# Load order of the first tiles and the source of the scaled identities in a fused attention and feed-forward kernel

## The chip, the cores and the metric

One core of a Trainium2 chip. The metric is the device time of one execution in microseconds (us). Single executions of one kernel here scatter by about 0.5 us to either side, a few by more, so times are medians of several. All runs that are compared are of the fast state. The span of a profile (first to last instruction) is 1.8 to 2.3 us shorter than the device time of that execution.

## The reference

```python
# attention: B, H, S, D = 4, 8, 768, 64
scores = q @ k.T / sqrt(D)                       # per head
keep   = (key position < 8) | (0 <= i - j < 96)  # 8 global keys, 96 local ones
scores += -slope[h] * dist                       # slope[h] = 2**-(h+1); dist 96 for global keys outside the band
x = softmax(where(keep, scores, -1e9)) @ v       # then heads side by side: x is 3072 x 512
# feed-forward: w_in 512 x 2048, w_out 2048 x 512
out = relu(x @ w_in)**2 @ w_out                  # float32
```

## The kernel before

The 3072 rows are 24 tiles of 128. For each of the first six tiles TensorE (PE) transposes q and k (for later tiles a DMA does). For every tile it makes scores (for the first three tiles with the bias added by a matmul of a *scaled identity* and the distance matrix), and multiplies the probabilities with v ("pv"). Two tiles make a block, and each block goes through eight slices of w_in ("s1": 8 matmuls per slice) and of w_out ("s2": 4 per slice). The weights are loaded once, a slice at a time. Every load but the q and k of tile 0 is issued by GpSimd and cast from fp32 to bf16 on the way; the same queue carries parts (q, k or v of one tile) and weight slices, and what stands behind waits for what stands ahead.

```python
def swdge(name, dst, src, t):              # one load of that queue
    nc.gpsimd.dma_start(out=dst, in_=src)
    issue[1] = max(issue[1], issue[0] + 3.3) + t
    issue[0] += 0.75 if name[0][0] == "w" else 0.88
    land[name] = issue[1] + 0.3 + min(max(0.1 * (issue[1] - 8), 0.0), 1.6)
...
load_part(0, 1); load_part(1, 1); load_v(0); load_v(1)         # q1 k1 v0 v1
...
for h in range(H):                                             # VectorE
    nc.vector.tensor_scalar_mul(sid[h], ident, float(slopes[h] / scale))
...
for w in "i0 T2 i1 T3 i2 o0 i3 o1 i4 o2 T4 i5 o3 i6 o4 T5 i7 o5 o6 o7".split():
    ...                                    # T: q, k, v of a tile; i: w_in slice; o: w_out slice
for name, at in list(land.items()):
    landed(name, at)                       # planned landing, an input to the static schedule
```

`land` is no more than a plan. When the program is built, a small list scheduler places all work on the engines, using these landing times; the order it finds is fixed. On the chip PE takes its work in this order and waits, by semaphore, for what really has not landed.

The softmax here doesn't subtract the row's maximum and nothing guards it: scores larger than these inputs give would overflow.

## Time and profile before

| what | before |
|---|---|
| device time, 3 runs | 214.84 us (214.77 to 214.9) |
| span of the profile | 213.1 us |
| PE busy | 205.5 us, 96% |
| transfers of GpSimd's queue | 79,200 packets, 13.37 MB |
| first s1 | starts at 14.9 us |
| the last idle time of PE that the profile shows | ends at 25.2 us |

The forty-slice row of PE in the prediction below is full except for the head and the end. A "chain" is followed back from the last instruction, and names at each step what it waited for last. A landing is read as issue time plus the time to landing in the list of DMA issues.

### The profile page before, as it was taken

To read this page: it belongs to the slowest core of one execution; us is meant where nothing else is said; L and a number is where in the kernel's file an instruction comes from. 1 tells how busy PE (TensorE), PEld (TensorE's weight loads), DVE (VectorE), ACT (ScalarE), POOL (GpSimd) and SP (SyncE) were. 2 spreads that over 40 slices of the span, in tenths; PEclk is the share of its full clock that TensorE was granted. 3 is DMA by queue.
4 is the path that set the end of the run, shared out by engine and by line. 5 is a ranking of instruction groups with operands and counts; after the bars stand their busy time and mean duration, and the time that the engine had idled before them with its cause. 6 is when DMAs were issued, how large, how long until landed. Compare 5 with 4: busy or idle time off the path is not lost.

```text
span 213.1 us, 5046 instructions
## 1 busy us (share of the span) xinstructions
PE 205.5 (96%) x1992; PEld 141.2 (66%) x1992; DVE 142.4 (67%) x383; ACT 117.5 (55%) x217; POOL 74.4 (35%) x91
## 2 busy tenths in 40 slices
PE   7968999999999999999999999999999999999994
PEld 3656677655676767666767667666767667676773
DVE  7756668752886768755867957855857857844640
ACT  6848476633763645753654754753754754733541
POOL 8986677531044134314314422422422400000000
PEclk9999999999999999999999999999999999999999
DMA  9999999999899999999999899799999992310202
GB/s 127 140 165 197 182 196 182 178 123 210 185 95 87 218 100 93 189 129 84 203 141 81 180 103 119 154 128 119 192 130 78 152 131 39 123 28 0 98 0 98
DMA packets 113702, 27.58 MB, mean 129 GB/s; under 512 B 104336, under 2 KB 110736, under 8 KB 113680
## 3 DMA queue, kind: packets, MB, share of 16 engines
q0 software_dynamic: 79200, 13.37, 81.4%
q1 hardware_dynamic: 34480, 13.90, 32.7%
q8 instruction: 15, 0.25, 0.5%
q14 instruction: 7, 0.06, 0.1%
HBM read 27.26 MB, written 6.29 MB: 157 GB/s over the span
## 4 chain that ended last, share of the span: by engine, by line
PE 87%; DMA 7%; POOL 4%; issue 0%; ACT 0%; POOLq 0%
PE hT L675 39%; PE acc L745 38%; DMA win<-in_moe_w_in_dram 7%; PE sc L449 5%; PE po L562 4%; POOL qk L193 2%; POOL v L193 1%; PE tr L372 0%; POOL win L193 0%; PE trx L625 0%; ACT o L304 0%; POOL pbi L246 0%; POOLq L246 0%; POOLq L813 0%
## 5 line engine op out<-in xcount | busy, mean ns | idle before, releaser
L675 PE MATMUL hT<-xT,win 128*128 128x256 bf16 x768 | 98.7, 273 | 0.4 <-DMA win<-in_moe_w_in_dram 0.2
L745 PE MATMUL acc<-wout,hs 128*128 128x512 bf16 (+1 forms) x400 | 98.1, 371 | 0.2 <-DMA wout<-in_moe_w_out_dram 0.2
L696 ACT ACTIVATE hr<-hT 128x512 f32<-128x512 f32 x96 | 57.4, 599 | 68.1 <-PE hT L675 67.0
L675 PEld LDWEIGHTS <-win 128*128 128x128 bf16 x768 | 72.8, 98 | 23.9 <-DMA win<-in_moe_w_in_dram 1.6
L708 DVE TENSOR_TENSOR hs<-hr 128x512 bf16<-128x512 f32 x96 | 65.9, 687 | 23.0 <-ACT hr L696 21.7
L745 PEld LDWEIGHTS <-hs 128*128 128x128 bf16 x400 | 36.5, 98 | 24.4 <-issue 0.4
L193 POOL DMA_DIRECT2D qk<-in_q_dram x23 | 20.6, 894 | 87.0 <-DVE qk L346 75.0
L495 ACT ACTIVATE esc<-sc 128x512 bf16<-128x512 f32 x78 | 42.1, 601 | 10.3 <-PE sc L449 10.3
L520 DVE TENSOR_TENSOR at<-esc,E 128x512 bf16<-128x512 bf16 x78 | 32.0, 422 | 8.0 <-ACT esc L495 6.9
L193 POOL DMA_DIRECT2D v<-in_v_dram x24 | 22.2, 924 | 2.4 <-DVE at L520 1.2
L590 DVE TENSOR_TENSOR x<-po,rs 128x256 bf16<-128x256 f32 x48 | 20.4, 425 | 1.7
L193 POOL DMA_DIRECT2D qk<-in_k_dram x23 | 20.5, 892 | 0.3 <-issue 0.2
L562 PEld LDWEIGHTS <-at 128*128 128x128 bf16 x352 | 16.8, 97 | 4.5 <-ACT at L495 0.6
L562 PE MATMUL po<-v,at 128*128 128x65 bf16 x352 | 18.6, 193 | 0.3 <-ACT at L495 0.3
L589 DVE RECIPROCAL rs<-po 128x4 f32<-128x4 f32 x48 | 8.7, 181 | 13.2 <-PE po L562 13.0
L449 PEld LDWEIGHTS <-qkT 64*128 64x128 bf16 x352 | 9.9, 94 | 8.4 <-issue 6.6
L306 DVE COPY o<-acc 128x512 f32<-128x512 f32 x11 | 7.6, 692 | 10.6 <-PE acc L745 10.6
L449 PE MATMUL sc<-qkT 64*128 64x128 bf16 x192 | 13.1, 219 | 0.4 <-DVE qkT L306 0.3
L304 ACT COPY o<-acc 128x512 f32<-128x512 f32 (+1 forms) x14 | 7.8, 555 | 6.7 <-PE acc L745 6.7
L449 PE MATMUL sc<-qkT,qkT 64*128 64x128 bf16 x160 | 11.3, 216 | 0.0
L193 POOL DMA_DIRECT2D win<-in_moe_w_in_dram x8 | 6.4, 794 | 1.7 <-DMA win<-in_moe_w_in_dram 1.1
L495 ACT ACTIVATE at<-sc 128x512 bf16<-128x512 f32 x10 | 5.3, 598 | 2.5 <-PE sc L449 2.5
(41 smaller groups left out, 58.2 us busy)
## 6 DMA issues: line engine op xcount, KB each, us to landing
out_dram<-o SPq DMA_DIRECT2D x23, 256.0 KB, 3.1
v<-in_v_dram POOLq DMA_DIRECT2D x24, 128.0 KB, 5.6
qk<-in_q_dram POOLq DMA_DIRECT2D x23, 128.0 KB, 4.7
qk<-in_k_dram POOLq DMA_DIRECT2D x23, 128.0 KB, 5.4
win<-in_moe_w_in_dram POOLq DMA_DIRECT2D x8, 256.0 KB, 8.6
wout<-in_moe_w_out_dram POOLq DMA_DIRECT2D x8, 256.0 KB, 8.8
qkT<-qk SPq DMA_TRANSPOSE x18, 3.5
xT<-x SPq DMA_TRANSPOSE x18, 3.8
```

Source lines behind the costliest of these rows:

```text
L193: nc.gpsimd.dma_start(out=dst, in_=src)
L304: nc.scalar.copy(dst, src)
L449: nc.tensor.matmul(out=tiles["sc", j, odd, g][:, at, :], lhsT=qkT[(j - kt) % NKT][half, 1, pair, :], rhs=qkT[j % NKT][half, 0, pair, :], s ...
L495: nc.scalar.activation(out=esc, in_=tiles.pop(("sc", j, odd, g)).rearrange("p a c -> p (a c)"), func=Act.Exp, scale=scale,)
L520: nc.vector.tensor_mul(at, tiles.pop(("esc", j, odd, g)), bias)
L562: nc.tensor.matmul(out=po[:, hi, :], lhsT=tiles["at", j, odd, g][:, at * P : (at + 1) * P], rhs=v_sb[kj][:, h, :], start=(i == 0), stop=(i ...
L589: nc.vector.reciprocal(rs, po[:, :, D : D + 1])
L590: nc.vector.tensor_tensor(out=x[:, 4 * hf : 4 * hf + 4, :], in0=po[:, :, :D], in1=rs.to_broadcast([P, 4, D]), op=Alu.mult,)
L675: nc.tensor.matmul(out=hT[:, c, :], lhsT=w_in_sb[s][:, kt, c * P : (c + 1) * P], rhs=tiles["xT", blk][:, kt, :], start=(kt == 0), stop=(kt ...
L696: nc.scalar.activation(hr, tiles.pop(("hT", blk, s)), Act.Relu)
L708: nc.vector.tensor_mul(hs, hr, hr)
L745: nc.tensor.matmul(out=tiles["acc", blk, sub, half], lhsT=hs[:, c, sub * P : (sub + 1) * P], rhs=w_out_sb[s][:, c, cols], start=(s == 0 an ...
```

## The change

Its intent: let the attention of the first four tiles run before any weights are needed, then have each weight slice serve two blocks as it lands; and make the scaled identities without holding GpSimd up. The landing table is fitted anew to the new order. The diff, cut to its core:

```diff
-    issue = [1.0, 5.0]
+    issue = [1.35, 4.6]
...
-        land[name] = issue[1] + 0.3 + min(max(0.1 * (issue[1] - 8), 0.0), 1.6)
+        late = [m for at, m in ((0, 0.5), (8, 0.8), (13.6, 1.9), (36, 2.8)) if issue[1] >= at]
+        land[name] = issue[1] + late[-1]
...
-    load_part(0, 1)
-    load_part(1, 1)
-    load_v(0)
-    load_v(1)
...
-        nc.vector.tensor_scalar_mul(sid[h], ident, float(slopes[h] / scale))
+        nc.vector.scalar_tensor_tensor(
+            out=sid[h], in0=ident32, scalar=float(slopes[h] / scale), in1=ident32,
+            op0=Alu.mult, op1=Alu.mult,
+        )
...
-    for w in "i0 T2 i1 T3 i2 o0 i3 o1 i4 o2 T4 i5 o3 i6 o4 T5 i7 o5 o6 o7".split():
+    for w in "q1 k1 v0 q2 k2 v1 q3 k3 v2 v3 i0 i1 i2 i3 o0 i4 T4 i5 o1 o2 i6 i7 o3 q5 k5 o4 o5 o6 o7 v5".split():
```

It has three parts: the *order* of the loads, the landing *table*, and the *identities*.

More of the change, by code (lines that the diff above doesn't have):

```diff
@@ L207 @@
             plain[n, j] = t_
-            land["qk"[n], j] = 4.15 + 1.1 * n
+            land["qk"[n], j] = 4.1 + 1.1 * n
     def load_v(j):
@@ L288 @@
         ones.update({j: o for j in js})
-    for w in "i0 T2 i1 T3 i2 o0 i3 o1 i4 o2 T4 i5 o3 i6 o4 T5 i7 o5 o6 o7".split():
-        kind, n = w[0], int(w[1:])
-        {"T": load_tile, "i": load_w_in, "o": load_w_out}[kind](n)
+    pieces = {
+        "T": load_tile, "i": load_w_in, "o": load_w_out, "v": load_v,
+        "q": lambda j: load_part(0, j), "k": lambda j: load_part(1, j),
+    }
+    for w in "q1 k1 v0 q2 k2 v1 q3 k3 v2 v3 i0 i1 i2 i3 o0 i4 T4 i5 o1 o2 i6 i7 o3 q5 k5 o4 o5 o6 o7 v5".split():
+        pieces[w[0]](int(w[1:]))
     for name, at in list(land.items()):
```

## The prediction

> **What bounds the kernel now.** I first read the page's busy shares and the row of forty slices, for which engine and when.
>
> ```profile
> span 213.1 us, 5046 instructions
> ...
> PE 205.5 (96%) x1992; PEld 141.2 (66%) x1992; DVE 142.4 (67%) x383; ACT 117.5 (55%) x217; POOL 74.4 (35%) x91
> ...
> PE   7968999999999999999999999999999999999994
> ...
> POOL 8986677531044134314314422422422400000000
> ```
>
> TensorE (PE) is the bound, and is short of work only in the first five slices (27 us) and in the drain of the last store. The change touches nothing after the loads of the first six tiles and the weights, so only the head can move. Next the table by stretches (PE's busy time is the second number):
>
> ```profile
> 4.00:8.00 4.00, 3.74 (x48) 2.75 (x48) 2.46 (x7) 3.52 (x10) 4.00 (x5) 1.00 2.04 137
> 8.00:12.00 4.00, 2.64 (x53) 1.84 (x48) 3.15 (x12) 2.65 (x6) 4.00 (x6) 1.00 1.90 151
> 12.00:16.00 4.00, 3.44 (x52) 2.70 (x52) 2.28 (x23) 1.83 (x4) 3.27 (x5) 1.00 2.08 169
> 16.00:20.00 4.00, 3.33 (x53) 2.46 (x54) 2.31 (x8) 3.12 (x7) 3.25 (x4) 1.00 1.51 195
> 20.00:24.00 4.00, 3.69 (x37) 2.51 (x38) 3.31 (x11) 2.53 (x6) 2.33 (x3) 1.00 1.35 200
> 24.00:28.00 4.00, 3.91 (x31) 2.62 (x30) 2.22 (x6) 2.07 (x4) 2.69 (x4) 1.00 2.03 173
> 28.00:48.00 20.00, 20.00 (x205) 14.27 (x202) 14.56 (x34) 11.93 (x22) 11.27 (x14) 1.00 1.78 168
> ```
>
> From 28 us PE is never idle. Before that busy time flatters it: an isolated block of 4 transposes counts 0.39 us, while in full flow the next block starts 0.23 us later. So I count streaming work. Starts in the timeline between 28 and 45 us give the cost of a block in full flow: 8 first matmuls ("s1" of one weight slice and block of two tiles) 0.87, 4 second matmuls ("s2") 0.86, 4 transposes 0.23, 8 probability-times-v matmuls ("pv", half a tile) 0.24, 16 score matmuls 0.55; 8 bias matmuls take about 0.45. From PE's first transpose (4.41) to 25.22 the kernel does 0.9 (fp32 transposes) + 6 x 0.23 + 5 x 0.45 + 3.5 x 0.55 + 7 x 0.24 + 4 x 0.23 = 9.06 us for the attention of tiles 0 to 3, and 4 s1 (3.48) and 2 s2 (1.72): 14.26 us of work in 20.81. **PE loses about 6.5 us there; this is the ceiling of any gain.** Being 2% faster needs 4.3 us of it.
>
> The chain of waits up to 27 us tells who causes it:
>
> ```profile
> 3.25 2.34 POOL v L193 x2
> 5.59 0.76 POOL win L193
> 6.34 1.76 POOL qk L193 x2
> 8.10 0.82 POOL v L193
> 8.92 7.17 DMA win<-in_moe_w_in_dram
> 16.09 0.28 issue
> 16.37 8.80 DMA win<-in_moe_w_in_dram
> 25.17 0.05 issue
> 25.22 1.81 PE hT L675 x15
> ```
>
> It is the load queue of GpSimd: the issues up to 9 us, then the transfers themselves. The last wait of PE for a load ends at 25.17, with the fifth w_in slice. The queue is a fixed stream: from issue plus time to landing I get w_in slice 2 at 19.9, w_out 0 at 21.2, w_in 3 at 22.6, w_in 4 at 25.2: one weight slice per 1.3 us; a q, k or v part takes 0.85 to 0.95. Two more landings that I use, from the list of DMA issues in narrow windows around their issue (v of tile 3 issued at 11.40, w_out slice 4 at 25.46):
>
> ```profile
> v<-in_v_dram POOLq DMA_DIRECT2D x1, 128.0 KB, 7.4
> ...
> wout<-in_moe_w_out_dram POOLq DMA_DIRECT2D x1, 256.0 KB, 8.8
> ```
>
> They land at 18.8 and 34.3.
>
> **The skill.** "SBUF — State Buffer", section "Who interferes with whom", says that tensor_scalar can take a two-port mode, in which it holds the port pair shared with GpSimd for the whole instruction; that a DMA issued by GpSimd needs GpSimd to write descriptors, so that it stalls meanwhile; and that a two-input op has no such mode. "VectorE: DVE Perf Modes", "What auto-detection actually checks", gives the fast modes to 16-bit, single-source, SBUF-to-SBUF operations. The eight bf16 scaled identities are that. The trace agrees in place and size:
>
> ```profile
> 3.22 2.37 POOL L193 DMA_DIRECT2D v<-in_v_dram  x2
> ...
> 3.40 1.30 DVE L273 TENSOR_SCALAR sid<-ident 128x128 bf16<-128x128 bf16 x8
> ```
>
> Two v issues take 2.37 us where later ones take 0.92 each: 0.53 us lost, beside the eight. "DMA: Bandwidth & Descriptors", "Queues, rings and completion order", says that descriptors of a queue start in ring order on each DMA engine. Landings that follow the issue order at these even steps agree. So the change reorders a stream, and does not shorten it.
>
> **The change part by part.**
> *Scaled identities.* Eight tensor_scalars (1.30 / 8 = 0.16 us) become eight two-input fp32 operations. The nearest row, the 256-column one of L259, is followed after 0.34 us; half the columns, about 0.21. Sum 1.7 us instead of 1.3: VectorE is free at about 5.1 instead of 4.7, just when its next job (5.05) starts, and the bias matmuls read the identities at 5.65: cost nearly 0. In return v's issue takes 0.9 and the whole load stream comes 0.5 us earlier.
> *Order of loads.* Until the end of w_in 0 the new queue is 10 parts and one slice. By content: the old stream had 10 parts and 2 slices landed at 18.8 (v of tile 3), so the new w_in 1 lands at 18.8 - 0.53 = 18.2, w_in 0 at 16.9, w_in 2 at 19.5, w_in 3 at 20.8, w_out 0 at 22.1, w_in 4 at 23.4. Tiles 2 and 3 land some 2 to 3 us earlier than now.
> What PE does with it, in the built order: attention of tile 1 is no longer followed by the waits for tile 2 (1.2 and 0.65 us now). With q and k of tile 2 at about 8.9 and 9.8, v 1 at 10.7, tile 3 at 11.5 to 15, PE finishes tiles 0 to 2 and the scores of tile 3 near 15, having waited some 2 us on copies, exponentials and loads. Then it has nothing until w_in 0: idle 15.2 to 16.9, a wait that takes the place of the removed ones. From there each slice serves two blocks of tiles instead of one: at 16.9 s1, pv of tile 3 between 17.8 and 19, at 19.5 and 20.8 the next s1, then block 1 on the same slices, tile 4's transposes, and so on, PE close behind the arrivals.
> *The new landing table* only makes the static order of PE fit these arrivals (the old one had w_in 1 at 14.8; it landed at 16.1).
>
> **The sum** I take where the new order is last bound by a load, w_out slice 3, the 25th in the queue. It has the content (13 parts, 12 slices) of the old w_out 4, 34.26 - 0.53 = 33.7. At that moment the new order has behind it 12 s1, 3 s2, all of tile 4's attention. The old one at 33.55 has done 10 s1, 4 s2, and lacks half of tile 4's pv and its last transposes. So the new one leads by 0.87 + 0.24 + 0.23 - 0.15 = **1.2 us**. From then on both are fed and PE-bound, so the lead stays to the end: 214.84 - 1.2 = 213.6 us.
>
> **The rivals.**
> (a) *Hidden anyway: the wait only moves.* The stream has the same bytes; w_in 0 comes 5 to 6 us later than now (11.1), and PE idles before it. If landings are half a microsecond later than I have them, or the attention phase is slowed by copies, little stays: 214.3 to 215. For it: the table written into the changed kernel puts a jump of about one microsecond at 13.6 and another 0.9 at 36; the second would delay the late w_out slices and eat 0.4 us of the lead. Against: by my tally two s1 more are done by 25 us.
> (b) *Larger gain.* The old stream lost more than the 0.53: between v 2 and w_in 1 landings lie 2.3 us apart instead of 1.3, and w_in 0 came 1.8 after v 1. If that came of mixing parts and slices, the new order is rid of about 1 us more, and PE, close behind the arrivals, takes all of it: 212.2 to 212.8. Against: the changed kernel's table still has such a jump.
> (c) *VectorE or ScalarE becomes the bound of the head* because four tiles' attention is now packed: between 8 and 16 us they are busy 5.4 and 4.5 of 8 us, so there is room; at worst a microsecond of the slack before 16.9 is used, which costs nothing. 214.
>
> **Range and chances.** Even the ceiling, 6.5 us, would have to be won by two thirds for 2%; I see a fifth. Range 212.3 (rival b) to 214.7 (rival a almost whole). Faster by over 2%: 4%; slower by 2% would need 4.3 us of new idle time in a head that has now 6.5: 2%; within 2%: 94%.
>
> **What would show it.** Right: the v issues near 3.2 us take 0.9 each, the scaled identities about 1.7 us in all; PE's idle time at 10.7 to 12.9 is gone, and a new one of 1 to 2 us ends with w_in 0 near 16.9; w_out 3 lands near 33.7; PE has no wait after some 37 us; PE's work and every other count are unchanged, and ends 1.2 us sooner. Wrong: w_in 0 landing after 18 (rival a) or before 16 (b); waits of PE for w_out slices beyond 37 us; v issues still slow; idle time of PE on copies or exponentials that outlasts the arrival of w_in 0.

## The result, and the profile after

The changed kernel took 213.6 us (6 runs, 213.01 to 214.0) against 214.81 us before in the same rounds; the ratio is 0.995, 95% interval 0.9928 to 0.9973. Ratios here and below are the mean time of one kernel's fast runs over that of the other's of the same rounds, so not quite the ratio of the medians quoted. It was run twice more later: 213.49 against 215.13 (0.9928, interval 0.9904 to 0.9952) and 213.74 against 214.94 (0.9946, interval 0.9914 to 0.9979). By the 2% rule this is "same"; the small gain is real.

The page of the changed kernel, the same lines:

```profile
span 211.5 us, 5047 instructions
...
PE 204.6 (97%) x1992; PEld 141.4 (67%) x1992; DVE 144.7 (68%) x388; ACT 115.4 (55%) x212; POOL 73.7 (35%) x91
...
PE   7978999999999999999999999999999999999994
...
POOL 8996567440404412422431431440431400000000
```

The span is 1.6 us shorter with the same 1992 matmuls. One digit in PE's row differs: only the third slice is fuller. The table by stretches (PE's busy time is the second number of a row):

```profile
4.00:8.00 4.00, 3.92 (x50) 3.11 (x48) 2.87 (x11) 3.50 (x10) 4.00 (x6) 1.00 2.28 151
8.00:12.00 4.00, 4.00 (x90) 3.42 (x86) 3.51 (x13) 3.30 (x8) 4.00 (x6) 1.00 2.37 154
12.00:16.00 4.00, 2.48 (x54) 1.86 (x50) 2.52 (x24) 2.56 (x7) 4.00 (x6) 1.00 1.65 179
16.00:20.00 4.00, 3.33 (x42) 2.99 (x43) 3.87 (x18) 2.77 (x5) 2.80 (x4) 1.00 1.39 199
20.00:24.00 4.00, 4.00 (x34) 2.88 (x32) 3.79 (x9) 1.79 (x3) 2.19 (x3) 1.00 2.04 172
24.00:28.00 4.00, 3.62 (x44) 2.96 (x44) 1.80 (x4) 2.17 (x4) 3.19 (x4) 1.00 1.36 200
28.00:48.00 20.00, 20.00 (x185) 12.88 (x180) 13.65 (x33) 9.17 (x17) 10.88 (x13) 1.00 1.70 187
```

The hole of 8 to 12 us is filled (4.00 instead of 2.64), and a new one stands at 12 to 16 (2.48 instead of 3.44). What PE waited for in it, from the list of waits between 4 and 50 us:

```profile
PE po L566 <- DMA v<-in_v_dram: 1.3, 1, 1.3
PE trx L629 <- DVE x L594: 0.8, 1, 0.8
PE tr L376 <- DMA qk<-in_q_dram: 0.4, 1, 0.4
```

So it waited for v of tile 2, for a normalization on VectorE, and for q of tile 4; not for w_in 0, which landed at 15.8, a microsecond before PE was ready for it. This is one execution: in the two later profiles of the same kernel (after_rep, after_pair) PE is busy for 3.39 and 3.31 of these 4 us, and its first s1 starts at 15.71 and 15.72, 0.05 us after w_in 0 landed. So which wait stands there changes from one execution to the next. In the timeline of the first profile, v's issue on GpSimd and the eight scaled identities on VectorE:

```profile
3.22 0.90 POOL L193 DMA_DIRECT2D v<-in_v_dram  x1
...
3.41 1.69 DVE L271 SCALAR_TENSOR_TENSOR sid<-ident 128x128 bf16<-128x128 f32 x8
```

The issue takes 0.90 us where it took 1.50 alone before (the two v issues together 2.37). The identities take 1.69 us, as predicted.

**Where the end is set.** Busy shares hide one thing that matters below. In the timeline of the kernel before, PE reaches the s2 of w_out slice 6 at 40.73 us:

```profile
40.34 0.41 PE L562 MATMUL po<-v,at 128*128 128x65 bf16 x8
40.73 1.02 PE L745 MATMUL acc<-wout,hs 128*128 128x512 bf16 x4
```

That slice landed at 40.69 (issued 31.91, 8.8 us to landing): PE began 0.04 us behind it, after a short wait that a busy time of 0.41 us covers. In the changed kernel the same is seen at w_out slice 3, which landed at 33.41:

```profile
33.14 0.39 PE L629 MATMUL trx<-ident,x 128*128 128x128 bf16 x4
33.45 1.02 PE L749 MATMUL acc<-wout,hs 128*128 128x512 bf16 x4
```

From that start to the end of the span it is 213.09 - 40.73 = 172.36 us before and 211.53 - 33.45 = 178.08 us after. These remainders come back in the other profiles of the same load order and table to 0.1 us: 172.29 to 172.36 from the s2 of w_out 6, and 178.03 to 178.08 from that of w_out 3 in six of seven (178.57 in fetch_shift, where PE waits 0.4 us for the transposed q and k of tile 6 later on). **The head is a stretch in which PE follows the load stream; it ends at a certain slice, and the rest has a fixed length.**

### The profile page after: what moved, and what is told of

The parts are those of the page before. It is cut to its first block, busy times and chain, and to the rows that moved or that the text cites. A ratio compares the mean times of both kernels' runs of the same rounds, so it can differ in the third digit from the quotient of the medians.

```text
span 211.5 us, 5047 instructions
## 1 busy us (share of the span) xinstructions
PE 204.6 (97%) x1992; PEld 141.4 (67%) x1992; DVE 144.7 (68%) x388; ACT 115.4 (55%) x212; POOL 73.7 (35%) x91
## 3 DMA queue, kind: packets, MB, share of 16 engines
q1 hardware_dynamic: 34480, 13.90, 31.7%
## 4 chain that ended last, share of the span: by engine, by line
PE 87%; POOL 6%; DMA 5%; issue 0%; ACT 0%; POOLq 0%
PE acc L749 39%; PE hT L679 38%; PE sc L453 5%; DMA qk<-in_q_dram 5%; PE po L566 4%; POOL qk L193 3%; POOL win L193 2%; POOL v L193 2%; PE tr L376 1%; POOL wout L193 0%; PE trx L629 0%; ACT o L308 0%; POOL pbi L247 0%; POOLq L247 0%; POOLq L817 0%
## 5 line engine op out<-in xcount | busy, mean ns | idle before, releaser
L193 POOL DMA_DIRECT2D v<-in_v_dram x24 | 21.5, 899 | 1.5 <-DVE rs L593 0.9
L566 PE MATMUL po<-v,at 128*128 128x65 bf16 x352 | 18.1, 193 | 1.3 <-DMA v<-in_v_dram 1.3
L453 PE MATMUL sc<-qkT,qkT 64*128 64x128 bf16 x160 | 11.3, 216 | 0.0
L193 POOL DMA_DIRECT2D wout<-in_moe_w_out_dram x8 | 5.8, 721 | 4.1 <-DMA win<-in_moe_w_in_dram 1.7
```

The source lines that it names most:

```text
L453: nc.tensor.matmul(out=tiles["sc", j, odd, g][:, at, :], lhsT=qkT[(j - kt) % NKT][half, 1, pair, :], rhs=qkT[j % NKT][half, 0, pair, :], s ...
L566: nc.tensor.matmul(out=po[:, hi, :], lhsT=tiles["at", j, odd, g][:, at * P : (at + 1) * P], rhs=v_sb[kj][:, h, :], start=(i == 0), stop=(i ...
```

## The experiments

All outputs were correct. Medians, with before from the same rounds:

| run | what it is | us | before | ratio (95% interval) |
|---|---|---|---|---|
| s_only | before, new identities | 213.90 | 214.59 | 0.9960 (0.9929 to 0.9990) |
| no_s | changed, old identities | 214.57 | 214.59 | 0.9985 (0.9954 to 1.0017) |
| no_o | old order, new table, new identities | 215.01 | 214.59 | 1.0008 (0.9971 to 1.0044) |
| no_t | new order, old table, new identities | 214.71 | 214.59 | 0.9998 (0.9965 to 1.0031) |
| after_rep | changed | 213.49 | 215.13 | 0.9928 (0.9904 to 0.9952) |
| s_onesrc32 | changed, one-input fp32 identities | 214.94 | 215.13 | 1.0004 (0.9975 to 1.0033) |
| ones_late | changed, 18 memsets later | 213.75 | 215.13 | 0.9946 (0.9921 to 0.9972) |
| before_rep | before | 215.24 | 215.13 | 1.0014 (0.9978 to 1.0050) |
| after_pair | changed | 213.74 | 214.94 | 0.9946 (0.9914 to 0.9979) |
| s_only_pair | before, new identities | 213.90 | 214.94 | 0.9948 (0.9923 to 0.9973) |
| fetch_shift | changed, longer PE program ahead | 213.87 | 214.94 | 0.9945 (0.9900 to 0.9990) |
| tuned | changed, order and table moved on | 213.74 | 214.94 | 0.9947 (0.9917 to 0.9977) |

**The clock.** One thing bears on all these ratios. Of the 33 executions of before in these rounds, 10 have a mean granted clock of only 0.992 (0 of 11, 6 of 11 and 4 of 11 in the three sets of rounds). Of the 6 of s_onesrc32, 3 have such a clock (0.989 to 0.992), of the 18 of the changed kernel 1 (0.990), of the 12 of s_only and s_only_pair none. before_rep's profile is such an execution: the granted clock is 0.65 between 12 and 16 us, 0.92 between 16 and 20, and full afterwards. These executions are about 0.9 us longer (before in the rounds of before_rep: means of 215.42 and 214.55 us). So a part of the differences in two of the three sets is that the dip came less often; whether the change brings this about, no run shows. Differences of the means of executions at full clock (0.997 or more):

| difference, us | at full clock |
|---|---|
| before to identities alone (s_only, s_only_pair) | 0.86, 0.85 |
| before to the whole change (after_rep, after_pair) | 1.30, 1.02 |
| before to the change without the identities (no_s, s_onesrc32) | 0.23, 0.15 |
| s_onesrc32 to after_rep | 1.14 |

Each is uncertain by about 0.5 us (0.7 for no_s), an estimate from the scatter of the executions. They leave the reading below as it is.

The theory from the prediction: the order gives more than half of the gain (0.7 us), the identities 0.5. Rival A: the identities are the whole gain. Rival B: the table, that is a better static order, is.

### The identities alone, twice

```diff
--- the kernel before
-        nc.vector.tensor_scalar_mul(sid[h], ident, float(slopes[h] / scale))
+        nc.vector.scalar_tensor_tensor(
+            out=sid[h], in0=ident32, scalar=float(slopes[h] / scale), in1=ident32,
+            op0=Alu.mult, op1=Alu.mult,
+        )
```

First run:

> The kernel before with only the scaled identities changed to the two-input fp32 form. Theory (the gain is the new load order; the identities only take 0.5 us out of the load stream): v issues near 3.2 us take 0.9 us each instead of 2.37 together, w_in slice 4 (before: landed 25.17) lands at 24.6 and PE's last load wait ends there, so about 0.5 us faster than before, 214.3. Rival A (the identities are the whole gain): 1.2 us faster, 213.6. Rival B (the landing table, that is the static order, is the gain): no change, 214.8.

Second run, in the same rounds as the whole change:

> The kernel before with the new identities alone, beside the changed kernel. Prediction's step: 0.5 us faster than before and 0.7 slower than the changed kernel. What the runs so far suggest instead: 0.7 to 1.2 us faster than before, and within 0.4 us of the changed kernel.

> The changed kernel, unchanged, in the same rounds as the next run, so that the two can be told apart. From the runs so far: identities alone -0.4%, whole change -0.5% and -0.7%, whole change without the identities -0.15% and 0.0%. If order and table add nothing of their own, this run and the next agree within 0.2 us; if they add the 0.7 us that the prediction gave them, this one is 0.7 us faster.

Measured: 0.7 and 1.0 us faster than before. In the shared rounds identities alone and whole change came out at 213.90 and 213.74 us, ratios to before 0.9948 and 0.9946. The interval on either is about 0.3% wide on each side, so the 0.7 us (0.33%) that the prediction gave to order and table is not excluded by this pair alone, but their best estimate is 0.02% (0.18 us between the means of all six executions of each, with the profiled ones, which the ratios leave out). Rival A fits. The timeline of the first run shows the stall gone (two v issues in 1.77 us, not 2.37) in the old order too:

```profile
3.22 1.77 POOL L193 DMA_DIRECT2D v<-in_v_dram  x2
...
3.40 1.69 DVE L273 SCALAR_TENSOR_TENSOR sid<-ident 128x128 bf16<-128x128 f32 x8
```

and PE again meets w_out slice 6 just as it lands (39.04), 1.65 us sooner than before:

```profile
38.70 0.41 PE L565 MATMUL po<-v,at 128*128 128x65 bf16 x8
39.08 1.02 PE L748 MATMUL acc<-wout,hs 128*128 128x512 bf16 x4
```

Its span is 211.37, so the remainder is 172.29; in the second run it is 211.96 - 39.65 = 172.31, and w_out 6 landed at 39.61. The old order ends its head at w_out 6 in all three, and w_out 6 lands 1.1 to 1.65 us earlier than in the first profile of before (0.7 to 1.25 earlier than in before_rep, 40.29).

### The change without the identities, in two ways

```diff
--- no_s: the changed kernel
+        nc.vector.tensor_scalar_mul(sid[h], ident, float(slopes[h] / scale))
--- s_onesrc32: the changed kernel
+        nc.vector.tensor_scalar_mul(sid[h], ident32, float(slopes[h] / scale))
```

> The changed kernel with the old scaled identities (one bf16 input). Theory: v issue near 3.2 us slow again (1.5 us instead of 0.9), every later load 0.5 us later, q of tile 4 lands at 25.0 instead of 24.5 and PE waits there; 214.1, so half a microsecond slower than the changed kernel and still 0.7 faster than before. Rival A: 214.8, all of the gain gone. Rival B: 213.6, no change.

> The changed kernel once more, unchanged, so that it stands in the same rounds as the next two runs, and for a second look at its landings. Expected: 1.2 us faster than before (213.6 if before is 214.8). If the landing of v of tile 2 (14.3 in the first profile, 2.6 us after the part ahead of it) and of q of tile 4 (24.5) stay late, they belong to the order; if they move, to chance.

> The changed kernel with the scaled identities made from the fp32 identity by a one-input operation. Theory (a one-input SBUF-to-SBUF operation holds GpSimd up, whatever its type): the v issue at 3.2 us takes again 1.4 to 1.5 us, and the loads land 0.5 us later, as in the run with the old identities; time 0.5 to 1.0 us over the changed kernel of these rounds. Rival (it is the bf16 source, or the second identity, that matters): v issue 0.9, time as the changed kernel.

Measured: order and table without the new identities are worth nothing that can be told from zero (ratios 0.9985 and 1.0004). In the rounds of after_rep, the one-input form costs 214.94 - 213.49 = 1.45 us (1.14 at full clock). The second run also settles what it is in the old form that hurts. From its timeline:

```profile
3.22 1.82 POOL L193 DMA_DIRECT2D v<-in_v_dram  x1
...
3.40 1.16 DVE L271 TENSOR_SCALAR sid<-ident 128x128 bf16<-128x128 f32 x8
```

The source is fp32, as in the change, but there is one input. VectorE is *quicker* with it (1.16 us instead of 1.69), and v's issue is the slowest of all forms, 1.82 us instead of 0.90. So it is the one-input form (here from SBUF to SBUF) and not the bf16 source. Not every such operation does it: in the profile of before a bf16 copy within E, also from SBUF to SBUF (VectorE, 7.70 to 8.22 us), runs beside issues of 0.91 and 0.92 us. w_in 0 lands at 16.3 (no_s) and 17.0 (s_onesrc32) instead of 15.7 to 15.8. In no_s PE again meets w_out 3 at its landing (33.40), and the remainder is 211.46 - 33.40 = 178.06, as in the changed kernel. That one profile lands w_out 3 no later than the changed kernel's (33.36 and 33.41), though w_in 0 to w_in 4 are all 0.6 to 0.8 us later: between the landings of w_in 4 and q of tile 4 lie 2.1 us in the changed kernel and 1.2 in this one. A single profile is thus no measure of the time; the six runs of no_s have a median 1.0 us above that of the first six of the changed kernel (other rounds, with before at 214.59 and 214.81).

### The order or the table alone

```diff
--- no_o: the kernel before with the new table and identities
-    issue = [1.0, 5.0]
+    issue = [1.35, 4.6]
-        land[name] = issue[1] + 0.3 + min(max(0.1 * (issue[1] - 8), 0.0), 1.6)
+        late = [m for at, m in ((0, 0.5), (8, 0.8), (13.6, 1.9), (36, 2.8)) if issue[1] >= at]
+        land[name] = issue[1] + late[-1]
... (left out: the planned landing of tile 0's q and k, and the identities as above)
--- no_t: the changed kernel with the old table (the same lines the other way round)
```

> The old load order with the new landing table and the new identities. Theory: the built order of TensorE is nearly that of the kernel before, so like the run with the new identities alone: 214.3. Rival A: 213.6. Rival B (the table is the gain): 213.6 as well, but then the run with the identities alone stays at 214.8.

> The new load order and the new identities with the old landing table. Theory: the table only changes small things in the static order, the time stays within 0.3 us of the changed kernel, 213.6 to 213.9. Rival B: 214.8, as before.

Both expectations missed. Both kernels have the new identities, and both are as slow as before: order and table must fit one another, and a table from elsewhere costs about as much as the identities give. (Of the 1.1 us between no_o and s_only some 0.4 lie outside the span: device time minus span is 2.3 us in no_o and 1.9 in s_only, which is not explained.) The list of PE's waits of no_t between 34 and 52 us shows two that the changed kernel does not have:

```profile
PE sc L452 <- DMA qkT<-qk: 1.0, 1, 1.0
PE acc L748 <- DMA wout<-in_moe_w_out_dram: 0.7, 1, 0.7
```

In its static order PE comes to w_out 4 before that has landed (36.75), and to the scores of tile 6 before their transposed q and k have (50.17). In no_o PE meets w_out 4 just as it lands, at 33.27, and its span of 212.42 leaves 179.15 us to go; s_only_pair is at the same s2 at 33.34, and has only 178.62 to go: with the foreign table less work had been put ahead of that slice. Rival B is half right: the table decides whether an order is worth anything. But the new order with its own table is no better than the old order with its own.

### A wait that was not worth removing

```diff
--- ones_late: the changed kernel
-            key=-1.0, ready=15.0,
+            key=-1.0, ready=22.0,
```

> The changed kernel with the 18 small memsets of the later v tiles planned at 22 us instead of 15, so that they no longer stand on VectorE ahead of the normalization of tile 2 (which ends at 16.6 in the changed kernel while w_in slice 0 landed at 15.8). Theory: the first w_in matmul starts at about 16.1 instead of 16.8, but PE then waits the longer for q of tile 4, and the time stays within 0.2 us of the changed kernel. Rival: VectorE bounds the head, and the 0.6 us come off the time.

The first s1 started right on the landing of w_in 0, earlier than in the first profile of the changed kernel (16.79):

```profile
15.58 1.05 PE L679 MATMUL hT<-xT,win 128*128 128x256 bf16 x8 [0.53 <-DMA win<-in_moe_w_in_dram]
```

In the unchanged kernel of the same rounds (after_rep) it starts at 15.71, though, so the later memsets brought some 0.1 us. The time did not fall (213.75 beside 213.49, ratios 0.9946 and 0.9928). The wait for VectorE, 0.8 us in the first profile and 0.3 in after_rep, was worth nothing that can be measured; PE waits for slices here (1.3 us for w_in, 1.1 for w_out).

### The late landings

> The kernel before, unchanged, for a second look at its landings. If w_in slice 1 lands again 2.3 us after v of tile 2, and w_in slice 4 near 25.2, the late landings belong to its order; if w_in slice 4 lands a microsecond earlier, they are chance, and so is that part of the gain.

Landings in us, of the two profiles of before and the three of the old order with the new identities:

| landing | before | before_rep | s_only | s_only_pair | no_o |
|---|---|---|---|---|---|
| v of tile 1 | 9.28 | 9.35 | 9.26 | 9.00 | 9.01 |
| w_in 0 | 11.09 | 11.20 | 10.47 | 10.40 | 10.37 |
| v of tile 2 | 13.80 | 13.90 | 13.18 | 13.12 | 13.08 |
| w_in 1 | 16.09 | 15.08 | 14.36 | 14.47 | 14.25 |
| q of tile 3 | 16.94 | 16.66 | 15.27 | 15.31 | 15.14 |
| w_in 4 | 25.17 | 24.78 | 23.49 | 24.09 | 23.66 |
| w_out 7, the last | 41.97 | 41.57 | 40.32 | 40.94 | 40.96 |

From w_in 0 to v of tile 2 the new identities bring the stream 0.6 to 0.8 us, close to the 0.60 by which v's issue is shorter. Then before loses 0.7 to 1.0 more, at w_in 1 in one look and at q of tile 3 in the other; none of the three others does, with the same mix of parts and slices. So it is not the mixing that costs it (rival b of the prediction). But they are late elsewhere: w_out 0 comes 1.84 us behind w_in 2 in s_only_pair and 1.76 in no_o (1.3 in before), and by w_out 7 these two are only 0.6 us ahead of before_rep, as much as the stall itself.

In before_rep the head did not end with a landing. w_out 6 was there at 40.29, but PE came to its s2 only at 40.97, behind in its work after the stretch of low clock; from there it is 172.33 us to the end as always.

What makes single loads late is partly seen. In the trace, 16 KB packets of the instruction queue run on the same DMA engines. The queue table of a window of the changed kernel (11.3 to 12.4 us) has one of them; columns are packets, MB and share of 16 engines:

```profile
q8 instruction: 1, 0.02, 5.4%
```

It took 0.95 us (5.4% of 16 engines in 1.1 us), where a part's packets of 128 bytes take 0.03 each. Such a packet comes each time PE has begun some 250 further instructions, weight loads and matmuls (counts of 235 to 283 at the first and 487 to 506 at the second, in all profiles but that of the next run). In the seven profiles with the changed kernel's load order, the landing that comes 0.5 to 1.7 us later than its place tells is v of tile 2 where the first packet starts at 11.4 us (two of two), and v of tile 3 where it starts at 11.9 to 12.8 (four of five). The last run of this group was to move the packet:

```diff
--- fetch_shift: the changed kernel
-    for i in range(NWARM):
+    for i in range(4):
         nc.tensor.matmul(out=warm, lhsT=zero[:, :P], rhs=zero, start=True, stop=True)
+    for i in range(30):
+        nc.tensor.matmul(out=warm[:16, :16], lhsT=zero[:, :16], rhs=zero[:, :16], start=True, stop=True)
```

> The changed kernel with some warm-up matmuls replaced by 30 tiny ones, so that TensorE's instruction stream is 52 instructions longer ahead of the first transpose. In all ten profiles a 16 KB packet of the instruction queue comes each time TensorE has begun another 250 or so instructions (235 to 267, then 487 to 506), occupies one DMA engine for 0.94 us, and the load landing 2 to 3 us later is a microsecond late. Theory (the packet delays the load): the first such packet now comes at about 10 us instead of 11.4 to 12.1, and the late landing moves with it, to k of tile 3 or v of tile 2 (due at 11.8 and 12.7), with v of tile 3 no longer the one; the second comes at 20 to 21 and hits w_out 0 or w_in 4. Rival (the late landing belongs to the change from parts to slices): v of tile 3 or v of tile 2 late at 14.3 to 15 as before, wherever the packet is. Time within 0.6 us of the changed kernel.

It missed its aim. The packet came at instruction 256 as meant, but PE was slower in the head now (the transposes of tile 0 are a group of 2.13 us instead of 1.29), so that this was at 11.6 us, not 10 (the edit need not be the cause of that: the same group takes 2.26 us in s_only_pair, which has the old warm-up); v of tile 2 was late (14.61), as it is with an early packet. That a packet delays a load fits most profiles and is shown by none. The expectation's "in all ten profiles" is too strong: the trace does not say which of the 16 engines a packet ran on, and in the old order with the new identities packets at 12.7 to 13.9 us delayed nothing near them.

### A further version

```diff
--- tuned: the changed kernel, memsets at 22 us, and
-        late = [m for at, m in ((0, 0.5), (8, 0.8), (13.6, 1.9), (36, 2.8)) if issue[1] >= at]
+        late = [m for at, m in ((0, 0.5), (8, 0.8), (13.6, 0.9), (21.5, 2.2), (36, 2.4)) if issue[1] >= at]
-    for w in "... v2 v3 i0 i1 i2 i3 o0 i4 T4 i5 o1 o2 i6 ...".split():
+    for w in "... v2 i0 v3 i1 i2 i3 o0 i4 o1 T4 i5 o2 i6 ...".split():
```

> The changed kernel with w_in slice 0 ahead of v of tile 3, w_out slice 1 ahead of tile 4, the 18 memsets at 22 us, and a landing table that is a microsecond earlier between 13.6 and 21.5 us, as the landings of the changed kernel are (w_in 0 at 15.7, planned 16.8). Theory (what is left in the head is PE waiting close behind the arrivals of slices): first w_in matmul at about 15 instead of 15.7 to 16.8, 0.3 to 0.7 us faster than the changed kernel. Rival (the stream's total, ending with the last slice near 40 us, sets the end whatever the order): same time.

The first s1 came at 14.65 us, one to two microseconds earlier than in the profiles of the changed kernel, and the time was that of the changed kernel (213.74 and 213.74). In the head the waits for slices grew, and a wait of 0.4 us for the transposed q and k of tile 6 appeared at 48.9 us, behind the end of the first loads:

```profile
PE sc L453 <- DMA qkT<-qk: 0.4, 1, 0.4
```

The rival is right: rearranging what PE does in the head did not help; of what was tried, only an earlier stream did. None of the versions tried beats the changed kernel by more than the scatter.

## Why the prediction was right in the number and not in its parts

- **What bounds the kernel, and the ceiling.** Right: only the head moved, and by far less than the ceiling.
- **The cost of the new identities.** Right: 1.7 us predicted, 1.69 measured, no wait for them, v's issue 0.9 us.
- **What the identities give, "the whole load stream comes 0.5 us earlier".** The mechanism was right (the one-input run shows it), the size was not. This term of the sum was 0.53 us; measured it is 0.7 and 1.0 us in the old order (s_only, s_only_pair; 0.86 and 0.85 at full clock) and 1.45 us in the new one (after_rep against s_onesrc32, whose stall is 0.3 us longer than the original's; 1.14 at full clock). The stall itself explains 0.6 (0.9 in s_onesrc32). The rest stays open: both streams of before were late again, at w_in 1 or q of tile 3, which is seen but not explained; and a part of the 1.0 and the 1.45 is the clock.
- **What the order gives.** This is the step that failed: "So the new one leads by 0.87 + 0.24 + 0.23 - 0.15 = 1.2 us" counted about 0.7 us of its own for the order. Measured in shared rounds it is 0.02% (214.94 x 0.0002 = 0.04 us; the intervals allow some tenths of a per cent), and without the identities 0.15% and nothing; at full clock 0.18, 0.23 and 0.15 us, all within the scatter. The error is in the baseline. The old order's progress was read from a profile that had the stall and the late w_in 1 in it, and only 0.53 us of this was taken to belong to the identities. With the identities changed, the old order is about as far.
- **Where the new order is last bound, "w_out slice 3", landing 33.7.** Right: it landed at 33.41 and 33.05 in the two profiles of the changed kernel in which no matmul record is missing, and PE began its s2 0.04 us later in both, with 178.08 and 178.07 us to go.
- **"From then on both are fed".** Wrong for the old order: it meets w_out 6 at 40.69 with 0.04 us to spare. Had I seen that, I would have known that the old order profits from an earlier stream just as directly.
- **The wait that takes the place of the removed one.** Its place was right (12 to 16.8 us), its cause only in part: in the first profile w_in 0 was there at 15.8 instead of 16.9, and PE waited for v of tile 2 and for VectorE; in the two repeats the wait ended with w_in 0, at 15.7. That the remainder from w_out 3 is the same in all three shows that this did not matter.
- **Rivals.** (a), the wait only moves, is what happened to the order. (b) was wrong in its cause. (c) happened in a small way and cost nothing, as stated there.
- **Range and chances.** The first result lies at the prediction, 213.6 us; the two repeats at 213.5 and 213.7.

So two errors of about equal size, of opposite sign, met in one sum. The right total was no evidence for the parts; only the runs that do one part alone told them apart.

## What to carry to other kernels

While a core starts up behind one queue of loads, whatever delays the issue of a load delays everything behind it, and eight small operations on an engine that is not critical can be worth more than a rearrangement of the whole head. Look for issues in the timeline that take longer than their kind, and see what the engine that shares a port runs at that moment. When two parts of a change act on the same stream, do not measure the second against a profile that still has the first one's loss in it: run each alone, in the same rounds.

## What the Trainium skill lacked or had wrong

- "SBUF — State Buffer", "Who interferes with whom": what it says of one-input operations and the descriptors of GpSimd's DMAs agrees with the v issue beside the identities: 0.90 us in all ten profiles with the two-input form, 1.50 and 1.82 in the four with a one-input form. It lacks how little it takes: eight operations of about 0.16 us (bf16, 1.30 us in all) lengthened one DMA issue from 0.90 to 1.50 us, eight of fp32 (1.16 us in all) to 1.82 us, and eight two-input ones (1.69 us in all) not at all.
- "Advanced Engine Details and Errata", "ISA Cache", has lines of 16 KB for 256 instructions, which agrees with the 16 KB packets of the instruction queue here, one per about 250 instructions of PE. No page warns that a load can land a microsecond late beside such a packet, which takes 0.95 us on one DMA engine (here 13.06 to 14.97 between two neighbouring v parts in a repeat of the changed kernel); no run here proves it to be the cause.
- No page has a term for the scatter of one kernel's landings between executions: w_out 3 of the changed kernel landed at 33.41 and 33.05, w_in 1 of the kernel before at 16.09 and 15.08.
